# A new order of issue and new buffer slots for a fused LSH attention and mixing kernel on one core

## The chip, the cores and the metric

The kernel runs on one core of one Trainium2 chip. The metric is device microseconds of an execution. The kernel before has a median of 711.25 us over 3 runs (711.11 to 713.57).

## What is computed

The reference has two parts. Attention runs for 4 batches, 8 heads, 768 positions and head size 64. Each query and key gets a 6-bit bucket from the signs of its product with `proj`; a query sees only the keys of its own bucket.

```python
mask = q_bucket[:, :, :, None] == k_bucket[:, :, None, :]
scores = np.where(mask, scale * np.matmul(q, k.transpose(0, 1, 3, 2)), -1000000000.0)
attn = np.exp(scores - np.max(scores, axis=-1, keepdims=True))
out = np.matmul(attn / (np.sum(attn, axis=-1, keepdims=True) + 1e-09), v)
```

The heads of a batch are laid side by side (768 x 512, called x below), and a mixing block follows:

```python
theta = x @ w_theta
y = einsum('ts,bsd->btd', w_tok_r, x * cos(theta)) + einsum('ts,bsd->btd', w_tok_i, x * sin(theta))
u = x + y
return u + np.maximum(u @ w_ch, 0.0)
```

## The kernel before, in words

Products are made to a precision near float32 out of float16 matmuls: an operand is split into a high and a low half, and a product takes three matmuls. So most stages have a step that makes the high half, one that subtracts it to get the low half, and groups of three matmuls.

**Attention.** For each batch and each pair of heads, `prep_qk` (line 443) loads queries and keys, scales and splits them and makes the rows of bucket bits (`sign`); `prep_v` (line 326) does the same for values. `assemble` (line 565) puts one head's operand together in `qk` by DMAs, and by four small steps that copy or mask the bit rows (`fbit`, `fmask`, lines 584 to 588), which any of ACT, DVE and POOL can do. `maxima` (line 605) computes scores of queries by keys (`qmax`, tile `sq`, PE), takes row maxima on DVE (`vmax`, tile `mc`, line 632), turns them on PE (`mtr`, tile `pmx`), and puts them into the operand by a DMA. `step` (line 677) then computes the scores again, keys by queries (`st`, PE), exponentiates them on ACT (`pf`, line 713), takes the high half on ACT (`p1`, tile `p`, line 719), the low half on POOL (`p2`, tile `p`, line 725), and multiplies by the values (`pv`, tile `po`, PE). One head of the first pair of each batch instead multiplies in float32 without a split. In batches 2 and 3 every second head takes another way (`turned`, line 804): scores `bt`, maxima `bm`, and a transposing DMA of the exponentials. `finish` (line 765) divides by the sums and writes x.

**Mixing.** `moe` (line 909) works on six row tiles of 128 rows for each batch. For each it makes high and low halves of x (`xh`, `xl`, tile `s_x`), turns them by a transposing DMA (`xturn`) and multiplies by `w_theta` (`proj`, tile `ps_th`). Angles are brought into range (`turns`, `rest`, `mag`), sine and cosine come from ACT (`trig`, lines 1086 and 1087), and x times these is split (`zf`, tile `f`, line 1098; `zh`, line 1103 or 1105; `zl`, line 1109). The token sum is 12 groups of 3 matmuls for each row tile (`y`, tile `py`), is added to x (`u`, line 1137), split and turned again (tiles `s_u`, `t_u`), multiplied by `w_ch` (`proj`, tile `ps_r`), and ends with `relu`, a sum (`fin`, line 1153) and a store. The very last row tile turns its data on PE instead (`turned_tile`, line 1007). The mixing of batch 0, 1 and 2 runs among the attention of the later batches; that of batch 3 is the tail.

**Weights** (`prep_weight`, line 236; `prep_wtok`, line 275) arrive as float64 bits and are converted on DVE, ACT and POOL (tiles `w_t`, `wf_t`, lines 212 to 230 and 296 to 301) in the first 260 us.

**The order.** None of these functions issues anything. Each one only registers steps (`op`): a name, the engines that may do it, the steps it depends on, and the buffer slots it uses. There are 4,219 steps. `issue_all` (line 111) first gives each slot a buffer number from the string `SLOTS`, 1,907 digits in the order in which the steps first name the slots; then it walks the string `ORDER` and issues the steps. An entry is an engine's letter (P is PE, A is ACT, D is DVE, G is POOL, S is the queue of DMAs on SyncE) and the step's number in base 36:

```python
for line in ORDER.split():
    e, x = line[0], int(line[1:], 36)
    o = ops[x]
    o.alts[ENGINES[e]][1]()
```

Each engine works through its own entries strictly in this order; a step whose input or buffer is not ready holds up all that stand behind it on the same engine. The first step that uses a buffer waits for all readers of the buffer's last contents.

Of the kernel before, what the change touches and what calls it, by code (L numbers as in the profile page):

```python
# [32 lines left out]
def lsh_attention_moe_kernel(ctx: ExitStack, tc: tile.TileContext, q, k, v, proj, w_theta, w_tok_r, w_tok_i, w_ch, out):  # L33
# [1233 lines left out]
    "0000000000000000000002100021012022110022100010000020001011000110011011101031000011021100221103021013311022111002030031313121300021"  # L1267
    "3010111320011200010110101001111110001110031000101203122211310003121001220331123000211121013010200010200003200010011112011010010101"
    "1031021003102213100203013110120123130010102001200121103021110210011031011101000000111001001211112313001212103100231212012110000333"
    "0221112100300011213100013000010010110010001111100011110012301121023013031111023200201303021111221130300110030022213130030110112121"  # L1270
    "1100100100100100000130111011100011100111001011203231130003111220303021002031032211311210000303220231110010130001230003100011001101"
    "0111010100111020120030020103221230112203010313103002221110110220230030111221201003013130111200011010001011013111010000110013311021"
    "0112213311222000301100031112202313132201001013020001311022030010130001100000001010110010103223102311000002212130322023111131000100"
    "0100301011021003202112313112100003011111022001101111111001200213011311122000003230100132310111232001032331032120022030101311010301"
    "1130210002200011011110011121032311100113301111000113113000222001300020102113103113302002201001203012130011113001330101101001301013"
    "3110010221031120003310113012212010012313210003200213100322000003300011200010300021110111011101111320033003220230003013130001032211"
    "3000032210110310112013102112103221010320111000001231111101100300113301301322001300011330120101221013100302310101111012121110300002"
    "2100331300011100003110110110101113031122010111220013032202011230101301002301110323010132100021012100101233111030001100011110000100"
    "2220113003131301133010221110021200230200013011122313300013020100231111103200001211020012110200111121012202210122000122110130020211"
    "0200100310210010320101101001021031012221012001201031121010222003011101000301110200003111000032113211010010211120212100300021002101"  # L1280
# [4 lines left out]
A6b D6v P6k D6l Sa9 A7b Sab P6i D6j A7d G7g A76 D6c G6d P6o A7f D6p P6s D6t Aaa S7c P6y D6z G6e P6m D6n P6q D6r P6w Aac Pad D6x P6f Dae G7e  # L1285
# [208 lines left out]
```

## Time and profile before

| | |
|---|---|
| median of 3 runs | 711.25 us |
| span of the profiled execution | 709.1 us |
| around the span, against the median | 2.15 us |
| PE busy / matmuls | 664.1 us / 6,212 |
| DVE busy | 599.4 us |
| ACT busy | 587.7 us |
| POOL busy | 419.8 us |

The span is that of one profiled execution, from its first to its last instruction. Busy time of an engine is the time in which at least one of its instructions runs. A matmul's row is longer than the time that it keeps the next one from starting: consecutive rows overlap, so busy times of PE are to be read by stretches and not by adding rows. An engine that lacks busy time in a stretch was waiting there.

### The profile page before, as it was taken

The numbers are of one execution on the slowest core, as the hardware profiler recorded it, in microseconds if no ns is written. First come the engines' busy times: TensorE is split into PE (matmuls) and PEld (weight loads), VectorE is DVE, ScalarE is ACT, GpSimd is POOL, SyncE is SP. The second block draws the span as 40 slices with busy tenths as digits, with TensorE's granted clock in tenths as the row PEclk, the third lists the DMA queues.
The fourth block names the chain that finished last, engine by engine and source line by source line (L and its number), as shares of the span: only waits on it lengthen the run. The fifth ranks groups of instructions, "written<-read, shape, count | busy, mean of one in ns | idle before, by whom it ended". The sixth has DMA issues, their size and how long they took to land.

```text
span 709.1 us, 16736 instructions
## 1 busy us (share of the span) xinstructions
PE 664.1 (94%) x6212; PEld 391.6 (55%) x6212; DVE 599.4 (85%) x1311; ACT 587.7 (83%) x1043; POOL 419.8 (59%) x411
## 2 busy tenths in 40 slices
PE   3899898899989989999999999999999999999997
PEld 1477675755444555655545565655545565654443
DVE  6899999999999999989998888889997777688222
ACT  7899899999968889999888999999897888875012
POOL 6457677366636567788738879767445778721001
PEclk9999999999999999999999999999999999999999
DMA  6654677657255633368824997888843576960123
GB/s 213 153 143 118 190 177 187 199 110 175 72 132 149 153 87 79 98 165 163 149 70 90 179 178 160 183 188 160 146 109 66 103 158 105 158 132 25 31 59 104
DMA packets 174561, 94.23 MB, mean 133 GB/s; under 512 B 148240, under 2 KB 164240, under 8 KB 174480
## 3 DMA queue, kind: packets, MB, share of 16 engines
q1 hardware_dynamic: 174336, 93.14, 58.1%
q8 instruction: 49, 0.80, 0.5%
q14 instruction: 32, 0.26, 0.1%
q10 hardware_dynamic: 144, 0.03, 0.1%
HBM read 32.53 MB, written 6.29 MB: 55 GB/s over the span
## 4 chain that ended last, share of the span: by engine, by line
PE 45%; DVE 19%; ACT 9%; issue 3%; DMA 0%; POOL 0%; ACTq 0%; DVEq 0%; POOLq 0%
PE py L77 18%; PE po L77 7%; PE ps_r L77 6%; PE st L77 5%; PE bt L77 3%; PE sq L77 2%; DVE f L1098 2%; PE ps_th L77 2%; DVE mc L632 2%; ACT pf L713 1%; ACT z L1086 1%; DVE bm L836 1%; DVE z L1064 1%; ACT pf L864 1%; ACT z L1087 1%
## 5 line engine op out<-in xcount | busy, mean ns | idle before, releaser
L725 POOL TENSOR_TENSOR p<-pf,p 128x512 f16<-128x512 f32 x180 | 226.4, 1272 | 84.8 <-ACT p L719 54.4
L77 PE MATMUL py<-z,wtk 128*128 128x512 f16 x864 | 205.4, 380 | 2.6 <-DVE z L1064 1.6
L632 DVE TENSOR_REDUCE mc<-sq 128x1 f32<-128x512 f32 (+1 forms) x216 | 143.6, 682 | 11.9 <-PE sq L77 10.5
L77 PEld LDWEIGHTS <-qk 120*128 120x128 f16 (+2 forms) x1056 | 98.4, 101 | 89.3 <-issue 28.8
L713 ACT ACTIVATE pf<-st 128x512 f32<-128x512 f32 x216 | 124.4, 590 | 14.8 <-PE st L77 9.3
L77 PEld LDWEIGHTS <-wtk 128*128 128x128 f16 x864 | 82.7, 98 | 93.3 <-issue 5.1
L77 PE MATMUL st<-qk 120*128 120x256 f16 (+1 forms) x576 | 127.0, 330 | 4.3 <-ACT pf L713 3.5
L878 POOL TENSOR_TENSOR late<-pf,late 128x384 f16<-128x384 f32 x96 | 93.6, 987 | 51.2 <-ACT late L872 34.9
L719 ACT ACTIVATE p<-pf 128x512 f16<-128x512 f32 x180 | 110.1, 627 | 6.4 <-PE po L77 4.8
L77 PEld LDWEIGHTS <-p 128*128 128x128 f16 x2160 | 85.2, 98 | 20.4 <-ACT pf L713 1.2
L77 PE MATMUL sq<-qk 120*128 120x512 f16 (+1 forms) x288 | 81.5, 337 | 12.4 <-DVE mc L632 5.0
L77 PE MATMUL po<-vv,p 128*128 128x65 f16 (+1 forms) x2160 | 92.0, 193 | 0.1
L864 ACT ACTIVATE pf<-bt,bm 128x384 f32<-128x384 f32 x96 | 60.7, 664 | 15.0 <-DVE bm L852 10.2
L77 PE MATMUL ps_r<-wch,t_u 128*128 128x512 f16 x276 | 68.2, 379 | 0.8 <-DVE rows L523 0.8
L77 PE MATMUL ps_th<-wth,t_x 128*128 128x512 f16 x288 | 68.2, 379 | 0.6 <-DVE rows L523 0.6
L836 DVE TENSOR_REDUCE bm<-bt 128x1 f32<-128x384 f32 x96 | 50.8, 548 | 14.3 <-PE bt L77 11.4
L872 ACT ACTIVATE late<-pf 128x384 f16<-128x384 f32 x96 | 47.9, 517 | 0.9
L1137 DVE SCALAR_TENSOR_TENSOR x<-py,sw,x 128x512 f32<-128x512 f32 x24 | 17.9, 744 | 31.9 <-PE py L77 31.8
L77 PEld LDWEIGHTS <-t_x 128*128 128x128 f16 x288 | 27.5, 98 | 30.4 <-issue 1.4
L77 PE MATMUL bt<-qk 120*128 120x384 f16 x192 | 43.7, 326 | 0.2
L1098 DVE SCALAR_TENSOR_TENSOR f<-x,zsc,z 128x512 f32<-128x512 f32 x48 | 40.6, 863 | 3.0 <-ACT z L1087 1.8
L77 PEld LDWEIGHTS <-t_u 128*128 128x128 f16 x276 | 25.8, 97 | 28.3 <-issue 2.1
(179 smaller groups left out, 1070.5 us busy)
## 6 DMA issues: line engine op xcount, KB each, us to landing
qk<-hl SPq DMA_DIRECT2D x62, 192.0 KB
raw<-in_k_dram SPq DMA_DIRECT2D x16, 384.0 KB
raw<-in_q_dram SPq DMA_DIRECT2D x16, 384.0 KB
vb<-in_v_dram SPq DMA_DIRECT2D x16, 384.0 KB
out_dram<-x SPq DMA_DIRECT2D x24, 256.0 KB
qk<-hl SPq DMA_DIRECT2D x62, 96.0 KB
w_t<-in_moe_w_tok_r_dram SPq DMA_DIRECT2D x6, 768.0 KB
w_t<-in_moe_w_tok_i_dram SPq DMA_DIRECT2D x6, 768.0 KB
```

The lines of the kernel that those rows point to most:

```text
L77: PE.matmul(out_, l, r, start=start, stop=stop, skip_group_check=True)
L632: DVE.tensor_reduce(col()[:, cs], u["sq"], AX.X, ALU.max)
L713: ACT.activation(wide("pf", spf, F32), u["st"], AF.Exp, scale=1.0 / (UNIT * math.sqrt(D)))
L719: ACT.activation(o_, u["pf"], AF.Copy)
L725: return lambda: eng.tensor_tensor(wide("p2", sp2, F16), u["pf"], u["p1"], ALU.subtract)
L836: DVE.tensor_reduce(part(y), w["w"], AX.X, ALU.max)
L864: ACT.activation(w["f"], w["w"], AF.Exp, bias=part(4), scale=part(3))
L872: ACT.activation(dst(0), w["f"], AF.Copy)
L878: return lambda: eng.tensor_tensor(dst(1), w["f"], dst(0), ALU.subtract)
L1064: DVE.scalar_tensor_tensor(t["zw"][1][:, tt], u["n"], t["mg"], res["ps"], ALU.subtract, ALU.subtract)
L1098: DVE.scalar_tensor_tensor(u["f"], tl[b][:, tt], zsc[:, b : b + 1], t["zw"][r][:, tt], ALU.mult, ALU.mult)
L1137: DVE.scalar_tensor_tensor(tl[b][:, to], res["py"], t["sw"][:, to : to + 1], tl[b][:, to], ALU.mult, ALU.add)
```

## The change

The two strings are replaced: every place in the walk, and 1,085 of the 1,907 slot digits. The set of steps, the functions behind them and the pools of buffers stay. Cut to its first and last lines:

```diff
 SLOTS = (
-    "0000000000000000000002100021012022110022100010000020001011000110011011101031000011021100221103021013311022111002030031313121300021"
...
-    "120211312003200011001102003011100031001111022112200120211003201120110220110011111003010"
+    "0000000000000000000001010120101212012202100010000022000101110010111010100111000031021113321123120000110332022011031020303111210031"
...
+    "132001310101031020000100103211100030100201002102011220121103101112110220110001111103000"
 )
 ORDER = """
-S5i A0 D1 S5g P5w D5x S64 A5j A5h P5k D5l A65 P66 D5m D5n D5o D5p A60 D67 A5z D5q D68 A62 D5r A5y S2 D5u A61 D5s D5v A63 P6u D69 D5t A77 D6a
...
-G35y P37y P37z P380 P381 P382 D370 P38l P38m P38n P383 P38o P38p P38q S2zc A32h P384 P385 P386 P387 P388 P37q P38r P38s D371 P38t D389 S372
-A38a P37r P37s P37t A37u G37v P373 P374 D38b S35z P38u P38v P375 S38c P376 D38w P38y A38z D390 S36m P38d P38e A377 D378 S379 G32i S32j P391
-P392 S37w P393 A394 D395 P38f S396 P38g A38h D38i S38j
+A0 S5i S5g S64 S2 S2k D1 A5j P5w A5h D5x P5k A65 D5l D5m G7g D5n D5o A5z D5p P66 D5q D5r D63 A5u G7d D67 D60 G7e A5s D68 D5v A61 D69 D5y Sab
...
+P37z P380 P381 P36y P37q D36z P37r A370 P382 D371 P383 S372 P384 P38k P38l P37s P37t P38m A37u P373 P374 P38n P38o P385 P386 P387 P388 P38p
+D389 P38q D37v A38a P375 D38b P38r S38c P38s P376 S37w P38t A377 S35z P38u G378 P38v P38d D38w S379 P38e P38y P38f A38z P38g D390 P391 A38h
+P392 G38i P393 S38j A394 D395 S396
 """
```

By engine, the ranks of the steps that stay on their engine move by this many places in its own queue: PE 3.8 on the mean (1,187 of 1,362 move, at most by 35), DVE 3.3 (at most 40), ACT 2.2 (18), POOL 1.1 (7), SP 1.4 (189 of 276, at most 15). 161 steps have another engine's letter. In brackets, how many of them stand among the first 217 us of matmul work in the list of before:

| from, to | steps |
|---|---|
| ACT to DVE | 47 (12): xh 13, fmask 11 (3), mag 9 (3), zh 6 (2), fbit 4 (2), qkh 2, fhi 1 (1), first 1 (1) |
| DVE to POOL | 41 (13): zl 16 (3), fbit 12 (4), fmask 7 (5), fin 5, wmul 1 (1) |
| DVE to ACT | 36 (10): zh 11 (2), fmask 8 (1), fbit 6 (3), xh 5 (1), mag 3, qkh 2 (2), first 1 (1) |
| POOL to DVE | 21 (8): zl 10 (3), fin 5, fbit 3 (2), wmul 2 (2), fmask 1 (1) |
| ACT to POOL | 11 (5): fbit 6 (2), fmask 5 (3) |
| POOL to ACT | 5 (1): fbit 4 (1), fmask 1 |

## Rows read from the trace of the kernel before

**Rows 1.** The page: span, and busy time of each engine with its share.
```profile
span 709.1 us, 16736 instructions
...
PE 664.1 (94%) x6212; PEld 391.6 (55%) x6212; DVE 599.4 (85%) x1311; ACT 587.7 (83%) x1043; POOL 419.8 (59%) x411
```

**Rows 2.** Windows: busy us (x instructions) by engine in seven stretches, TensorE clock, DMA.
```profile
0.00:20.00 20.00, 7.85 (x24) 2.71 (x24) 12.99 (x34) 14.41 (x23) 12.89 (x35) 1.00 0.71 209
20.00:114.00 94.00, 87.76 (x883) 63.45 (x883) 89.46 (x193) 86.32 (x163) 60.71 (x55) 1.00 0.60 166
114.00:147.00 33.00, 29.13 (x310) 21.77 (x311) 32.60 (x78) 32.62 (x61) 16.61 (x16) 0.95 0.63 159
147.00:256.00 109.00, 100.49 (x866) 54.95 (x866) 106.48 (x196) 94.44 (x165) 63.74 (x53) 0.98 0.49 124
256.00:400.00 144.00, 137.63 (x1384) 80.29 (x1383) 132.69 (x293) 133.45 (x237) 102.17 (x94) 1.00 0.59 124
400.00:640.00 240.00, 238.08 (x2454) 139.52 (x2453) 198.71 (x483) 212.18 (x379) 158.30 (x158) 1.00 0.73 144
640.00:709.00 69.00, 63.19 (x296) 28.95 (x294) 26.50 (x40) 14.31 (x22) 5.34 (x5) 1.00 0.18 50
```

**Rows 3.** Waits of PE: for whom, us in total, times, longest.
```profile
PE pb L77 <- DMA raw<-in_q_dram: 5.4, 1, 5.4
...
PE sq L77 <- DVE mc L632: 5.0, 10, 1.0
```

**Rows 4.** Timeline near 255.6 us: start, us, engine, instruction, idle before.
```profile
255.60 0.38 PE L77 MATMUL sq<-qk 120*128 120x512 f16 x1 [0.88 <-DVE cinv_ch L181]
```

**Rows 5.** Timeline near 253 us, DVE and POOL.
```profile
252.97 1.72 DVE L980 SCALAR_TENSOR_TENSOR s_u<-x,su,s_u 128x512 f16<-128x512 f32 x1
...
252.99 1.16 POOL L725 TENSOR_TENSOR p<-pf,p 128x512 f16<-128x512 f32 x1 [1.32 <-ACT p L719]
```

**Rows 6.** Groups of DVE by form, 0 to 256 us: busy us, mean ns, idle.
```profile
L632 DVE TENSOR_REDUCE mc<-sq 128x1 f32<-128x512 f32 x84 | 56.5, 680 | 1.0 <-PE sq L77 0.6
...
L1098 DVE SCALAR_TENSOR_TENSOR f<-x,zsc,z 128x512 f32<-128x512 f32 x12 | 11.6, 964 | 0.8 <-ACT wg_ch L222 0.7
...
L586 DVE TENSOR_SCALAR qk<-rows,pp 24x384 f16<-24x384 f16 x13 | 7.4, 567 | 0.4
...
L301 DVE TENSOR_TENSOR wf_t<-wf_t 128x768 f16<-128x768 f32 x12 | 13.4, 1127 | 0.1
...
L226 DVE SCALAR_TENSOR_TENSOR wf_t<-wf_t,scw 128x1536 f32<-128x1536 f32 x6 | 12.0, 2002 | 0.1
```

**Rows 7.** Tiles, whole run: shortest/median/longest ns, first and last start, forms.
```profile
L632 DVE TENSOR_REDUCE mc<-sq x216: 637/681/693, 13.3 to 585.2; 128x1 f32<-128x512 f32 x73, 128x2 f32<-128x512 f32 x35
...
L1098 DVE SCALAR_TENSOR_TENSOR f<-x,zsc,z x48: 730/747/1751, 171.3 to 651.4; 128x512 f32<-128x512 f32 x48
...
L586 DVE TENSOR_SCALAR qk<-rows,pp x27: 312/397/1221, 27.6 to 588.5; 24x384 f16<-24x384 f16 x27
...
L301 DVE TENSOR_TENSOR wf_t<-wf_t x12: 936/958/1941, 84.5 to 238.7; 128x768 f16<-128x768 f32 x12
...
L226 DVE SCALAR_TENSOR_TENSOR wf_t<-wf_t,scw x6: 1797/1818/2687, 74.8 to 234.3; 128x1536 f32<-128x1536 f32 x6
```

**Rows 8.** Groups of POOL, whole run: busy us, mean ns, idle and its releasers.
```profile
L725 POOL TENSOR_TENSOR p<-pf,p 128x512 f16<-128x512 f32 x180 | 226.4, 1272 | 84.8 <-ACT p L719 54.4 <-PE po L77 8.1 <-issue 7.4
...
L586 POOL TENSOR_SCALAR qk<-rows,pp 24x384 f16<-24x384 f16 x4 | 6.3, 1566 | 0.4
```

**Rows 9.** Timeline of the tail.
```profile
694.83 1.23 SPq L984 DMA_TRANSPOSE t_u<-s_u  x1
...
699.30 0.64 PEld L77 LDWEIGHTS <-t_u 128*128 128x128 f16 x4
...
704.85 0.69 ACT L1150 ACTIVATE rl<-ps_r,qu 128x512 f32<-128x512 f32 x1 [0.61 <-PE ps_r L77]
...
705.57 0.69 DVE L1153 TENSOR_TENSOR x<-rl,x 128x512 f32<-128x512 f32 x1 [0.60 <-ACT rl L1150]
```

More of the change, by code (lines that the diff above doesn't have):

```diff
@@ L1271 @@
[L1271 to L1278, printed above, removed]
@@ new lines @@
+    "1021110300011000010010101101110001100311011111000023033203111123100003121231102130110011311100200011000002300010011010001100011110"
+    "1110030323001202310023130011120231132311000031013001102131110030011021011100010101100110100311112210311312000002231322013302001011"
+    "1210003110201130012000121000030010110010001101001010110122001333120000111122120013330011133001221101102200203013200110223130011320"
+    "1111300123100110001000010011011011130010300123200110223132012320001111200110122300300112130112230130001213211000230001010010101101"
@@ new lines @@
+    "0111110100121113000012113012031212130001330221000213103013103101023013110101233032112021110000013000010101012101111000012001213101"
+    "0030211210202123313100021110212210001003021133121001211002031000331000220002211110010002103022112211110020212331211100201200333101"
+    "1100300000021003212112313101120013001111011001220111001011301320201021011033313111133001102021020001233301022121132231001100110210"
+    "0233210000100003110011100111033331011013301020333121112330020010210121130003001103322111220113201110113011101001010110000111101020"
@@ new lines @@
+    "1003302021111032013121103123100201002330300001201112110123301002011133200011100032110110100001133110111212030331121101020020033300"
+    "1110122032003121001000012332103113011221111030001330110001100200120312111033111103021020033112131002100200021113231021120110201001"
+    "3301021100010000023010011001001122011313103110021210011110001322023300001032012011001230112302001231110323111032001201100100111201"
+    "2110002212330100001111220013132110002010231101321302301311100301302210011000001211320010113000121120122112021012010312012031112200"
@@ L1282 @@
+    "2130032111100011010030110200310110103110221020120231012201111011031002201002101100010210201131000100221131020210102021311101100120"
+    "132001310101031020000100103211100030100201002102011220121103101112110220110001111103000"
 )
 ORDER = """
[L1284 to L1285 removed]
@@ new lines @@
+Phd Ahj Pgz Pem Dh0 Ad Gkf D2y Sgj Pep Ahk Dke Ahe Ghl Dfq Pgv Ab Phn Dgw Sh Pi2 Ahf Dkg Pes Aho Dc Sf Ghg Ai3 Ph3 Phs Dh4 Ahp Pgt Pdz Aht
+Dgu Pki Ghq Pi7 Ak0 Det Dh7 Phx Deu Ph8 Dkj Phh Ai8 Pku Ahu Dha Po7 Dh9 Shc Dkv Pkk Ahy Pih Ghv Do8 Ai4 Phm Do9 Dkl Pky A2z Pic Doa Shb Gi5
+Dob De0 Ahz Pk1 Doc De1 Phr Sl6 Aid Dk2 Dod Pkw De Gi0 Poj Ala Dkx Ai9 Phw Aii Pir Dk3 Dk4 Dkz Pkm Aie Gia Pi1 Dkn Sg Ais Pkq Pio Dl9 Aij
+Gl8 Pko Pi6 Dk5 Dl7 Aip Gif Pj9 S32 Doe Dok Ak6 Piq Dkr Gik Aoh Dkp Pj6 Pib Dk7 Aja Pks Pig Aj7 Doi Gk8 Piu Aof Pix Dkt St9 Pit Aiv Di A30
@@ new lines @@
+Px9 Ay0 Gxi P10f A4a Pxe Dzw D10g Szy Pxu A49 P2no Dzx D4v A14c Gxn D10i P2np A2e D4b P2o4 Axr D4w S4o Pyv D2f A14e P10b Gxs P2o5 A2g Dyw
+Dyx Pxj Dyy D10c Pxo Axv S2i Dyz P2o6 D2h Az0 P10d P2nq D13s Ay5 S2j P10y A4x Dz1 Axw P118 Ay1 P107 Gxx Pxt D108 S18j A119 P2o7 S14b D4p
+A11a P2o8 Gy2 D10e Ay6 P10t D4q A4r P2o9 A10u Gy7 D2nr P109 A4y P2oa D10a Szz A14d P10j G4z P2op D2iq A14f Gz2 P2oq A18k P105 Pxy Py3 A4s
+P11i A10z Py8 D2io D106 P2or A10v A11j Dy9 P2os D4t G11b A110 D50 Dya P10l P2ob A2mi D51 D52 D10m Gz3 P53 A2lv P11s P113 D2lw G10w A11t Pz4
```

272 lines of the change are left out of this document (130 added, 142 removed).

## The prediction

> **What bounds the kernel now.** I read the page first [rows 1]. PE (the matmul engine) is busy for 664.1 of 709.1 us, so 45.0 us of the span are without a matmul. A new order cannot shorten the matmuls; it can only win from those 45.0 us, or lengthen them. Next come the windows [rows 2], where the reader should look at PE and DVE side by side. PE lacks 12.2 us in the first 20, 6.2 from 20 to 114, 3.9 from 114 to 147, 8.5 from 147 to 256, then only 6.4 from 256 to 400 and 1.9 from 400 to 640, and 5.8 in the tail. DVE is the reverse: from 20 to 256 us it lacks only 4.5 + 0.4 + 2.5 = 7.4 of 236 us (97% busy), and after 400 it has room (198.7 of 240). So there are two regimes: up to 256 us DVE is the engine that is always full and PE waits for it here and there; after 256 PE is full itself. The waits agree: apart from the first load (5.4 us, once) PE waits longest and most often with the score matmul `sq` behind the row maximum `mc` on DVE, 5.0 us in 10 waits [rows 3].
>
> How far DVE binds can be counted along the orders. For a matmul group, add the durations of all DVE instructions up to the last one that it needs, and subtract the matmul work that stands ahead of it on PE: PE must have been idle at least that long. In the order of before the largest value is at the `sq` group that begins at 255.60 us [rows 4]: 240.7 us of DVE against 216.4 us of matmuls, 24.3 us. (The DVE sum agrees with the windows: 13.0 + 89.5 + 32.6 + 106.5 = 241.6 up to 256 [rows 2].) PE's real idle time by then is 30.8 us. What the floor doesn't explain is DVE's own idle time, 7.0 us in the first 20 and 7.4 after.
>
> Against this reading speaks the Trainium skill (Perfetto Trace Analysis, Identifying the Most-Contended Engine): it says that matmul busy time is a poor measure of the distance to the limit, that weight-load busy time is a better one, and that the engine with the highest occupancy is the one to improve. By that rule PE would have room (weight loads 55%) and DVE, 85%, would bind throughout. The windows side with the rule up to 256 us and against it from 400 to 640, where PE has 1.9 us left.
>
> **The change part by part.** All 4,219 steps stay; 161 change engine, nearly all others stand a few places from where they stood (on PE by 3.8 places on the mean, at most 35), and 1,085 of 1,907 buffer slots differ.
>
> *DVE's floor.* Counting the new order by the same durations (a step that changes engine gets the mean of its kind on its new engine), the largest value is 241.4 us of DVE against 218.2 of matmuls: 23.1 us. **Gain 1.2 us.** Of it 0.9 is work that leaves DVE ahead of that point (23 steps leave, 20 come: the table of the change has them); the rest is order. Bounds: 0 (the mean durations don't hold) and 1.2.
>
> *DVE beside POOL.* The same DVE instruction takes different times. At 252.97 us `s_u` takes 1.72 us beside a POOL subtraction [rows 5]. In the first 256 us the mean of `f` is 964 ns, of the mask copy `qk` 567, of the two weight steps `wf_t` 1127 and 2002 [rows 6]; their shortest are 730, 312, 936 and 1797 [rows 7]. The surplus is 12 x 0.23 + 13 x 0.26 + 12 x 0.19 + 6 x 0.21 = 9.7 us. The row maxima `mc`, which read PSUM, lie between 637 and 693 in all 216 cases [rows 7]; so it is instructions that read SBUF alone which suffer. I therefore counted, for each POOL step up to the 218th us of matmul work, which DVE steps the list sets beside it: SBUF-only ones for 56.6 us of 145.8 before, 49.9 of 156.0 after. That is 12% less time, or 18% less as a share. **Gain 12 to 18% of 9.7, taken as 1.5 us.** The other end is a loss: POOL gets 11.4 us more work ahead of 256 us, 7.9% of its 144.6, and if collisions grow with POOL's time, 0.8 us are lost. Upper end 1.7.
>
> On these collisions the Trainium skill (SBUF — State Buffer, SBUF: two separate sides) says that VectorE and GpSimd share one port pair as an exclusive lock, held for a whole instruction, and that the loser stands still until the other ends. The `s_u` row agrees in kind: 1.72 us is 1.0 over the 0.7 that steps of its size take elsewhere (`f` in rows 7), and POOL's subtraction takes 1.16. By the lock alone, more POOL work is more lost DVE time, and this part would be a loss.
>
> *DVE's own idle time, 7.4 us.* For each matmul group I took its latest producer on another engine and asked how much matmul work the list sets between the two, less the producer's duration; negative values are matmul work that is lacking. Summed from 0 to 20, 120 and 220 us of matmul work they are 22.8, 18.7 and 12.1 us for the order in which before really started its steps, and 28.3, 24.5 and 9.5 for the new list. The early part is no better, the later one is. I take **0**, between -7.4 (all of it goes) and +4.5 (it doubles in 20 to 114).
>
> *PE's waits from 256 to 640, 8.3 us [rows 2].* The same count gives 15.6 and 9.7 before (220 to 400, 400 to 600 us of matmul work), 9.2 and 10.9 after: 20% less. **Gain 1.7 us**, between 8.3 and -3.
>
> *ACT and POOL.* ACT loses 10.7 us of work and POOL gains 30.2 over the span. Both have cover: up to 640 us POOL is busy for 16.6 of 33 us at its emptiest and 102.2 of 144 at its fullest [rows 2]. If the cover went, a step moved to POOL would cost what it holds up the subtraction `p` behind it (third rival). ACT alternates between the exponential and the sine 12 times in either order, so table loads cost the same.
>
> *SP's queue.* 189 of 276 steps change rank, by 1.4 places on the mean, and carry their DMAs with them. No DMA step stands over 15 places away, and PE's only long wait for one is the first load. Cost 0.
>
> *The tail.* Before ends with the project of row tile 4, after with that of tile 5; either way the last matmul is followed by one ACT step and one DVE step of 0.69 us each [rows 9] and a store. Tile 4's last sum moves to POOL (1.27 us, as the equally wide `p` [rows 8]): covered by the 12 matmuls left, 12 x 63.2/296 = 2.6 us [rows 2]. Tile 4's way from its token sum through ACT, DVE and a transposing DMA had slack; now 9 groups of 3 matmuls (27 x 0.2135 = 5.8 us) stand beside 3 steps of about 0.7 and a DMA that is issued at 694.83 and read at 699.30 [rows 9], at most 4.5. At worst 0.8 us are uncovered; I take 0.
>
> **Sum.** -1.2 - 1.5 + 0 - 1.7 + 0 = -4.4. The profiled execution spans 709.1 us, which is 2.15 below the median of the runs, 711.25; so 704.7 spanned, and **706.8 us** as a median, 0.6% faster. Half a per cent (3.6 us) is about what a measurement of this kernel can tell from no change, so the forecast lies only just outside.
>
> **The rivals.**
> *The stalls go too.* If the new order also takes 5.0 of DVE's 7.4 us and 3 more of the 6.6 us left of PE's waits after 256, the time is 706.8 - 8.0 = 698.8. For it: from 120 us of matmul work on, producers stand earlier. Against: ahead of that they don't.
> *DVE's total is what counts.* By mechanism: DVE stays 97% full, and what is gained at one group is waited for at the next. DVE's work falls by 1.7 us over the span, so 709.6; if POOL's extra work lengthens collisions by 0.8 as well, 710.4. This is what the skill's rule on the most-contended engine and its port lock would give together. For it: the floor moves by only 1.2. Against: PE's windows after 256.
> *POOL holds up the subtraction.* 18 steps go to POOL ahead of 256 us; a mask step takes 1.57 us there against 0.57 on DVE [rows 6, 8]. The subtraction `p` behind it, which the next `po` matmuls read, has 84.8/180 = 0.47 us of idle time ahead of it [rows 8], so each such step can delay PE by 1.1 us where PE is right behind. Four of them eat the gain; from 8 on the kernel is slower by over 0.5%. With 9 it is 706.8 + 9.9 = 716.7. Against: POOL is half empty from 114 to 147 us.
>
> **How the numbers follow.** Forecast as summed 0.42, stalls gone too 0.13, DVE's total 0.30, POOL 0.15. Faster by over 0.5% (below 707.7) are the first two: 0.55; the third is no change: 0.30; the fourth slower: 0.15. The range is to leave out 2 in 10: it ends at 699.5, short of the centre of the best case, and at 714.0, which takes in the forecast with DVE's idle time doubled (711.3) and the third rival's lighter half.
>
> **What would show it.** Right: up to 256 us PE lacks some 3 us less than 30.8, DVE stays over 96% full, and the means of `f` and `wf_t` fall. From 256 to 640 PE lacks 6 to 7 us in place of 8.3. Wrong: DVE's busy time in that stretch falls by over 5 us (collisions were worth more), or its idle time changes by more than 3 (the order itself counts), or PE's waits name POOL's `p` or `qk`.

## The result, and the profile after

The new kernel takes **717.68 us** as a median of 10 executions (715.4 to 723.88); the kernel before, run beside it on the same chip, 712.64 (711.11 to 715.85). The ratio is 1.0072, 95% interval [1.0047, 1.0098]: slower by 5.0 us, where 4.4 us less were forecast and 714.0 was the upper end of the range. The profiled execution spans 715.3 us, against 709.1 before. One execution of e12 and one of e15 below fell into a slower state and are left out of their times.

The page of the new kernel answers to [rows 1]:

```profile
span 715.3 us, 16724 instructions
...
PE 670.2 (94%) x6212; PEld 393.8 (55%) x6212; DVE 607.2 (85%) x1302; ACT 581.0 (81%) x1026; POOL 453.6 (63%) x437
```

PE has the same 6,212 matmuls and is busy for 6.1 us longer with them. POOL has 33.8 us more (30.2 by the durations of before) and ACT 6.7 less; DVE, which by the durations of before should have 1.7 us less, has 7.8 more. The windows, in the stretches of [rows 2] (columns as there: busy us and instructions of PE, PEld, DVE, ACT, POOL, then TensorE's clock, DMA share, GB/s):

```profile
0.00:20.00 20.00, 7.88 (x26) 3.10 (x26) 12.73 (x34) 13.03 (x21) 14.90 (x35) 1.00 0.70 234
20.00:114.00 94.00, 89.74 (x880) 64.37 (x880) 87.09 (x186) 82.46 (x156) 62.43 (x60) 1.00 0.53 144
114.00:147.00 33.00, 29.38 (x277) 22.22 (x276) 30.81 (x73) 29.29 (x53) 15.64 (x17) 0.90 0.73 193
147.00:256.00 109.00, 98.79 (x874) 54.06 (x873) 105.49 (x187) 95.81 (x165) 67.98 (x52) 0.98 0.55 127
256.00:400.00 144.00, 138.05 (x1387) 79.94 (x1384) 135.88 (x299) 129.70 (x232) 109.38 (x99) 1.00 0.56 120
400.00:640.00 240.00, 237.07 (x2459) 138.63 (x2457) 203.00 (x481) 209.51 (x373) 174.28 (x172) 1.00 0.73 144
640.00:715.30 75.30, 69.31 (x323) 31.44 (x321) 32.16 (x45) 21.21 (x30) 9.01 (x7) 1.00 0.20 51
```

Read DVE first. From 20 to 256 us it lacks 6.9 + 2.2 + 3.5 = 12.6 us, where it lacked 7.4; it is 95% full in place of 97%. PE lacks 30.2 us up to 256 (30.8 before) and 8.9 from 256 to 640 (8.3 before). So PE does not stand still longer; it works longer. Look at the clock in 114 to 147: 0.90, in [rows 2] 0.95.

The cleanest place to compare is one matmul that waits for DVE in both kernels: the total of the channel weights, `pw_ch`. First its row in the kernel before and the window up to it, then the same of the new kernel:

```profile
251.91 0.38 PE L77 MATMUL pw_ch<-wcol_ch,ones 128*128 128x1 f32 x2 [0.97 <-DVE wcol_ch L258]
...
0.00:251.91 251.91, 222.03 (x2065) 141.32 (x2066) 237.54 (x489) 224.29 (x400) 150.94 (x153) 0.99 0.57 153
```

```profile
259.27 0.38 PE L77 MATMUL pw_ch<-wcol_ch,ones 128*128 128x1 f32 x2 [0.82 <-DVE wcol_ch L258]
...
0.00:259.27 259.27, 228.24 (x2068) 144.85 (x2068) 239.33 (x488) 223.46 (x397) 164.14 (x164) 0.98 0.57 148
```

It comes 7.4 us later. By DVE's account, 1.8 us of that are more work (237.5 to 239.3) and 5.6 more time without work (14.4 to 19.9; counted instruction by instruction, as the expectations below do, 14.8 to 20.3). By PE's account, 1.1 us are more idle time (29.9 to 31.0) and 6.2 more busy time for 2,068 matmuls in place of 2,065. At the usual pace of each form of matmul the work ahead of this one is 214.6 us in place of 213.7, so 5.3 of the 6.2 are the same work done at a slower pace (the half clock, shown below, can account for 4.9 of them at most).

(In [rows 4] the largest value of the prediction's floor was at the scores at 255.60 us; in the new kernel it is at `pw_ch`.) Behind it 1.2 us come back in this execution: the two executions differ by 6.2 us in span, the medians by 5.0. In a second profile of the new kernel (e16 below) `pw_ch` begins at 258.83 us, and the time behind it is 457.6 us, 457.2 in the kernel before. So the loss lies ahead of this matmul.

What DVE waited for from 20 to 256 us (for whom: us in total, times, longest), before and after:

```profile
DVE mc L632 <- PE sq L77: 0.9, 3, 0.4
```

```profile
DVE mc L632 <- PE sq L77: 5.9, 14, 1.5
DVE wf_ch L212 <- DMA w_ch<-in_moe_w_ch_dram: 1.3, 1, 1.3
```

Most of what is new is the row maximum `mc` waiting for scores `sq` (4.0 us in 11 waits in the second profile). [Rows 3] has the other direction, PE's scores waiting for the maxima; it rose too, and a wait of PE for transposing DMAs is new (whole span):

```profile
PE sq L77 <- DVE mc L632: 8.1, 17, 1.8
...
PE ps_th L77 <- DMA t_x<-s_x: 1.7, 4, 0.7
```

The groups of DVE up to 256 us, as [rows 6], and the subtraction on POOL over the span, as [rows 8]:

```profile
L632 DVE TENSOR_REDUCE mc<-sq 128x1 f32<-128x512 f32 x82 | 54.7, 679 | 3.9 <-PE sq L77 3.5
...
L301 DVE TENSOR_TENSOR wf_t<-wf_t 128x768 f16<-128x768 f32 x12 | 12.4, 1037 | 0.1
L226 DVE SCALAR_TENSOR_TENSOR wf_t<-wf_t,scw 128x1536 f32<-128x1536 f32 x6 | 12.3, 2055 | 0.1
L1098 DVE SCALAR_TENSOR_TENSOR f<-x,zsc,z 128x512 f32<-128x512 f32 x12 | 11.1, 921 | 0.2
...
L1109 DVE TENSOR_TENSOR z<-f,z 128x512 f16<-128x512 f32 x9 | 7.7, 852 | 0.1
...
L586 DVE TENSOR_SCALAR qk<-rows,pp 24x384 f16<-24x384 f16 x11 | 6.6, 603 | 0.3
...
L1067 DVE TENSOR_SCALAR z<-z 128x512 uint32<-128x512 uint32 x6 | 4.5, 747 | 0.0
```

```profile
L725 POOL TENSOR_TENSOR p<-pf,p 128x512 f16<-128x512 f32 x180 | 228.9, 1287 | 94.3 <-ACT p L719 71.1 <-issue 8.0 <-PE sq L77 5.0
```

Two of these groups, which [rows 6] does not show, in the kernel before:

```profile
L1109 DVE TENSOR_TENSOR z<-f,z 128x512 f16<-128x512 f32 x9 | 6.1, 681 | 0.0
...
L1067 DVE TENSOR_SCALAR z<-z 128x512 uint32<-128x512 uint32 x3 | 1.2, 416 | 0.0
```

The collisions beside POOL did not go; they moved. `f` fell by 43 ns for each of 12 and L301 by 90 for each of 12, 1.6 us; L226 rose by 53 for each of 6, `qk` by 36 for each of 11, L1109 from 681 to 852 (9 instructions) and L1067 from 416 to 747 (6): together 4.2 us more. Other groups fell, among them L216 and L212 of `wf_t` by 148 and 118 ns for each of 6. Over all forms of DVE instructions that both kernels have, the changes of the means up to 256 us add up to 0.6 us more (7.7 up, 7.1 down).

The end is that of [rows 9], with the other row tile: one ACT step, this DVE step, and the store.

```profile
711.74 0.69 DVE L1153 TENSOR_TENSOR x<-rl,x 128x512 f32<-128x512 f32 x1 [3.29 <-ACT rl L1150]
```

### The profile page after: what moved, and what is told of

Its sections match the earlier page's. It is cut to its first block, busy times and chain, and to the rows that moved or that the text cites. A ratio compares the mean times of both kernels' runs of the same rounds, so it can differ in the third digit from the quotient of the medians.

```text
span 715.3 us, 16724 instructions
## 1 busy us (share of the span) xinstructions
PE 670.2 (94%) x6212; PEld 393.8 (55%) x6212; DVE 607.2 (85%) x1302; ACT 581.0 (81%) x1026; POOL 453.6 (63%) x437
## 4 chain that ended last, share of the span: by engine, by line
PE 56%; DVE 28%; DMA 6%; ACT 5%; issue 3%; POOL 1%; SPq 0%; DVEq 0%; ACTq 0%; POOLq 0%
PE py L77 19%; PE po L77 11%; PE st L77 7%; DVE mc L632 7%; PE ps_r L77 6%; PE bt L77 4%; PE sq L77 4%; DVE f L1098 3%; PE ps_th L77 2%; DVE z L1064 1%; PE pb L77 1%; DVE hl L473 1%; DMA qk<-row 1%; DMA t_x<-s_x 1%; DVE wf_t L226 1%
## 5 line engine op out<-in xcount | busy, mean ns | idle before, releaser
L725 POOL TENSOR_TENSOR p<-pf,p 128x512 f16<-128x512 f32 x180 | 228.9, 1287 | 94.3 <-ACT p L719 71.1
L632 DVE TENSOR_REDUCE mc<-sq 128x1 f32<-128x512 f32 (+1 forms) x216 | 144.2, 680 | 18.4 <-PE sq L77 17.4
L77 PE MATMUL st<-qk 120*128 120x512 f16 (+1 forms) x576 | 128.6, 331 | 5.6 <-ACT pf L713 3.6
L878 POOL TENSOR_TENSOR late<-pf,late 128x384 f16<-128x384 f32 x96 | 95.4, 1005 | 36.3 <-ACT late L872 29.4
L77 PEld LDWEIGHTS <-p 128*128 128x128 f16 x2160 | 86.7, 99 | 19.5 <-issue 4.1
L77 PE MATMUL sq<-qk 120*128 120x512 f16 (+1 forms) x288 | 83.0, 340 | 15.1 <-DVE mc L632 8.1
L77 PE MATMUL po<-vv,p 128*128 128x65 f16 (+1 forms) x2160 | 93.9, 195 | 0.4 <-POOL p L725 0.4
L1153 POOL TENSOR_TENSOR x<-rl,x 128x512 f32<-128x512 f32 x8 | 10.1, 1268 | 56.2 <-ACT rl L1150 56.2
L1098 DVE SCALAR_TENSOR_TENSOR f<-x,zsc,z 128x512 f32<-128x512 f32 x48 | 44.6, 942 | 0.4
L1109 POOL TENSOR_TENSOR z<-f,z 128x512 f16<-128x512 f32 x20 | 26.6, 1334 | 28.9 <-ACT z L1103 17.4
```

Of the source, the lines that this page charges most:

```text
L77: PE.matmul(out_, l, r, start=start, stop=stop, skip_group_check=True)
L632: DVE.tensor_reduce(col()[:, cs], u["sq"], AX.X, ALU.max)
L725: return lambda: eng.tensor_tensor(wide("p2", sp2, F16), u["pf"], u["p1"], ALU.subtract)
L878: return lambda: eng.tensor_tensor(dst(1), w["f"], dst(0), ALU.subtract)
L1098: DVE.scalar_tensor_tensor(u["f"], tl[b][:, tt], zsc[:, b : b + 1], t["zw"][r][:, tt], ALU.mult, ALU.mult)
L1109: return lambda: eng.tensor_tensor(t["z"][r, 1][:, tt], u["f"], t["z"][r, 0][:, tt], ALU.subtract)
```

## The experiments

Each was timed against the kernel before on the same chip, whose median was 712.9 to 713.6 us. "DVE without work" is counted up to `pw_ch` (the expectations call it the wall matmul): 14.8 us before, 20.3 in the new kernel. Times are medians; a ratio comes from all executions that are compared and need not be the quotient of two medians (for e18 that would be 1.0025).

### The three parts of the change, one alone

The order with the old engines, and the other way round:

```diff
 e1, from the new kernel: the 161 steps back on their engines
-G7d D67 D60 G7e A5s D68
+A7d D67 A60 G7e D5s D68
 e2, from the kernel before: the 161 steps on their new engines
-A60 D67 A5z D5q D68 A62 D5r A5y
+D60 D67 A5z D5q D68 A62 D5r D5y
```

> The new list and the new slots, but each of the 161 moved steps back on its old engine. If the engine moves cost the time (POOL 30 us fuller, its subtractions later), the time is within 1.5 us of the kernel before. If the new order itself costs it, the time stays 4 to 6 us above before. By the trace of the changed kernel the second is likelier: PE's new waits up to 130 us are for DVE row maxima and ACT exponentials, none for POOL.

> The old list and the old slots with the 161 steps on their new engines. Engine moves to blame: 4 to 6 us above before. Order to blame: within 1.5 us of before.

Measured: e1 746.02 us (ratio 1.0462, [1.0444, 1.0481]), e2 742.95 (1.0437 [1.0406, 1.0468]). All four forecasts fell. Either part alone costs 30 to 33 us, six times what both cost together, so neither can be called the cause of the 5 us. An order fits one choice of engines.

Then the buffer slots. The prediction gave them no term at all.

```diff
 e9, from the kernel before: slots of the new kernel where they are free
-30101113200112000101101010011111
+31211103000110100101101011001100
 e10, from the new kernel: slots of before where they are free
-10211103000110000100101011011100
+30111103200112000101101010011111
```

> The order and the engines of before, with the buffer slots of the new kernel wherever the old order leaves them free (1,052 of the 1,907 slots differ from those of before, 395 had to be chosen anew). Slots theory (other buffers make a step wait for another reader, and that is where the 5.0 us come from): 715 to 718 us, ratio 1.004 to 1.007, and DVE without work up to the wall matmul goes from 14.8 us towards 20. Order theory (the slots only follow the order): within 1.5 us of before, ratio 0.998 to 1.002, and DVE without work at 14 to 16 us.

> The order and the engines of the new kernel, with the slots of before wherever the new order leaves them free (358 of 1,907 had to be chosen anew, where the new kernel differs in 1,085). Slots theory: most of the loss goes, 713 to 715 us, ratio 1.000 to 1.003. Order theory: as the new kernel, 716 to 719 us, ratio 1.005 to 1.009, and DVE without work up to the wall matmul stays at 19 to 22 us.

Measured: e9 770.21 (1.078 [1.0742, 1.0817]), e10 751.09 (1.0527 [1.0508, 1.0546]). Both expectations fell, by far more than the whole change. DVE without work is 37.8 us in e9 and 29.1 in e10. PE waits for its score buffers' last readers, in e9 and then in e10 (waits of the whole span):

```profile
PE st L77 <- ACT pf L713: 21.9, 23, 2.0
PE sq L77 <- DVE mc L632: 14.0, 20, 2.1
```

```profile
PE sq L77 <- DVE mc L632: 24.3, 38, 2.5
PE st L77 <- ACT pf L713: 8.8, 16, 1.9
```

So which buffer a step gets decides as much as where it stands, and a set of slots fits one order. Both runs price a mixed set, since 395 and 358 slots had to be chosen anew. In the new kernel, slots and order fit better: its row for `st` behind `pf` is 3.6 us in 4 waits (3.5 in 6 before), and for `sq` behind `mc` the 8.1 shown above (5.0 before). How much of these 3.1 us more the slots hold, and how much the order, these runs don't show.

### Stretches of the new list in the old one

```diff
 entries of ORDER (4,219), with their slots
 e3:  1 to 923 new, the rest old            (until 120 us of matmul work)
 e4:  1 to 923 old, the rest new
 e5:  1 to 1563 old, the rest new           (until 220)
 e6:  924 to about 1590 new, the rest old
 e7:  1564 to 3890 new, the rest old        (220 to 560)
 e12: 205 to about 640 new, the rest old    (20 to 80)
```

> The new list (order, engines, slots) until 120 us of matmul work have been issued, the old list after. In the traces PE's idle time of the new kernel is 4.0 us ahead of the old one's at that point and 6.2 at the end. If the loss is made there and carried along: 3 to 5 us above before. If what is lost early is won back in a stretch where DVE has room: within 1.5 us.

> The complement: the old list until 120 us of matmul work, the new list after. If the loss is made early: 1 to 3 us above before (the 2.2 us that the traces add after that point). If it is made anywhere by the denser order: 4 us or more above before.

> The old list until 220 us of matmul work, the new one after. Theory: the loss arises where DVE binds, because DVE itself has to wait there more often than before (19.9 us idle up to 256 us against 14.5), so the part after 220 costs little: within 1.5 us of before, or 1 us faster, since PE's waits from 220 to 400 were 0.8 us shorter in the new trace. Rival, the loss is spread over the later list as well: 2.5 us or more above before, as in the complement before (4.7 us with the new list from 120 on).

> The new list only between 120 and 220 us of matmul work, the old one on both sides. Theory: 2 to 4 us above before, since this is the DVE-bound stretch in which the runs so far differ. Rival, the loss is spread: at most 1 us above.

> The new list only between 220 and 560, where PE binds; old before and after, so without the new tail, which costs 1.2 us in both traces that have it. Theory: 0 to 2 us faster than before. Rival: 1 us or more slower, because a seam or the later list costs time of its own.

> The new list (order, engines, slots) only from 20 to 80 us of matmul work, the one stretch in which PE lost less time in the new kernel than in any kernel with the old list (2.0 against 2.5 to 4.1 us), and the list of before ahead of and behind it (26 slots chosen anew). If that stretch is better in itself: 711 to 712.5 us, ratio 0.997 to 0.999, faster than both kernels. If what it saves is given back behind it, or at its two seams: 713 to 716 us, ratio 1.000 to 1.004.

| kernel | us | ratio, 95% interval |
|---|---|---|
| e3 | 714.21 | 1.0018 [0.9999, 1.0036] |
| e4 | 716.72 | 1.0065 [1.0044, 1.0087] |
| e5 | 716.84 | 1.0048 [1.0034, 1.0063] |
| e6 | 715.86 | 1.0039 [1.0018, 1.0060] |
| e7 | 720.52 | 1.0108 [1.0084, 1.0132] |
| e12 | 721.25 | 1.0113 [1.0085, 1.0140] |

e3 came as if the loss were won back later, e6 as its theory has it; in e4, e5 and e7 the second case or the rival came, and e12 lies above both of its cases. No stretch of the new list is shown to be faster than the old one, and no single one costs all that the whole list costs: e3, e6 and e5 cost 1.3, 2.8 and 3.4 us by their ratios, 7.5 in sum (with intervals of 1 to 1.5 us each way) where the whole costs 5.1. e12 shows why such sums don't hold: 60 us of the new list, in which it lost least, cost 8 us when they are set in, more than the whole new list. A seam needs slots of its own (26 in e12, 49 in e7, where PE loses 7.2 us, over its matmuls at their usual pace, behind 560 us of matmul work and 1.7 in the kernel before; up to 1.5 of it in a stretch at half clock from 621.6 to 625.0 us) and leaves the steps behind it out of turn. The profiles say where such a cost sits: behind `pw_ch` e5 takes 461.0 us, where the kernel before takes 457.2 and the new one 456.0 and 457.6. So e5's loss belongs to its seam or to what follows it, and does not speak for a loss of the whole list there. These six runs don't divide the loss.

### Scores earlier, maxima later

```diff
 e8, from the new kernel: 114 scores up to two places earlier on PE
-P6m A7a Pad G7f D6n P6w
+P6m A7a P6w Pad G7f D6n
 e11, from the new kernel: 99 maxima one place later on DVE
-D6r P6k D6l Aac P6s D6c P6y
+D6r P6k Aac P6s D6c D6l P6y
```

> The whole new list, but up to 220 us of matmul work the score matmuls that DVE reduces (sq) stand up to two places earlier on PE, 114 of 127 of them. In the new trace DVE waited for sq 5.9 us between 20 and 256 us in 14 waits, against 0.9 in 3 before. If these waits are what was lost: 2 to 5 us faster than the new kernel, about level with before. If they only mirror PE's own lateness: PE then waits for the two buffers of sq instead, and the time stays or rises by some us.

> The new kernel, in which 99 of the 127 row maxima up to 220 us of matmul work stand one place later on DVE. Theory that DVE stands still since the list sets the row maximum too close behind its scores: the 17.4 us that DVE waits for the scores fall by 4 us or more, DVE without work up to the wall matmul falls from 20.3 to 16 to 18 us, 713 to 716 us. Rival, that DVE's maximum and the next scores follow each other through two banks, so that a later maximum only holds up the scores: PE's waits for the maxima rise from 8.1 us to 11 or more, DVE without work stays at 20 or over, 718 to 723 us.

Measured: e8 722.05 (1.0129 [1.0104, 1.0155]), e11 726.44 (1.0180 [1.0162, 1.0197]). In both the waits that were aimed at became less, and the time more. Whole span, DVE and PE, for e8 and then e11; the new kernel has 17.4 us in 33 waits and 8.1 in 17:

```profile
DVE mc L632 <- PE sq L77: 12.9, 22, 1.4
...
PE sq L77 <- DVE mc L632: 17.5, 27, 2.1
```

```profile
DVE mc L632 <- PE sq L77: 13.0, 23, 1.4
...
PE sq L77 <- DVE mc L632: 15.5, 17, 2.5
```

Scores and maxima hand each other two banks. Whether the scores are set earlier or the maxima later, the wait goes over to the other engine: 4.5 us less on DVE are 7 to 9 more on PE. A wait in the table is thus no loss that can be taken out by moving its step everywhere. In e8 the second case of its expectation came. For e11 the rival's waits came (15.5 us on PE, 22.7 of DVE without work), and a time above even its range.

### The clock

In the first profile of the new kernel the full clock (2.4 GHz) comes later and the half clock (1.2 GHz) lasts longer. A score row at half pace and the first at full pace, before and after (start, us; a score matmul of 120x512 takes 0.63 us at half pace and 0.38 at full; the second row of the kernel before is a pair of half the size):

```profile
25.45 0.63 PE L77 MATMUL sq<-qk 120*128 120x512 f16 x1
...
26.80 0.38 PE L77 MATMUL sq<-qk 120*128 120x256 f16 x2
```

```profile
29.11 0.63 PE L77 MATMUL sq<-qk 120*128 120x512 f16 x1
...
32.92 0.38 PE L77 MATMUL sq<-qk 120*128 120x512 f16 x1
```

The clock's records begin at 26.0 and 31.9 us. Behind that, windows ahead of and in the first stretch at half clock, of the kernel before and of the new one:

```profile
128.50:142.00 13.50, 11.84 (x102) 9.62 (x102) 13.33 (x30) 13.28 (x27) 5.69 (x6) 1.00 0.68 213
142.00:145.40 3.40, 3.40 (x22) 2.12 (x22) 3.34 (x8) 3.40 (x8) 2.48 (x3) 0.50 0.54 104
```

```profile
114.00:127.50 13.50, 9.88 (x110) 5.80 (x109) 13.34 (x37) 12.63 (x23) 10.19 (x9) 1.00 0.76 186
127.50:134.30 6.80, 6.80 (x70) 6.24 (x69) 6.76 (x13) 5.98 (x8) 1.00 (x1) 0.50 0.71 184
```

PE has less to do ahead of it (9.9 of 13.5 us, before 11.8), then is at half clock for 6.8 us in place of 3.4, and full all through. DVE's longest wait for scores comes right behind it. DVE's row, and PE's of the work that stood ahead of the scores:

```profile
135.97 0.69 DVE L632 TENSOR_REDUCE mc<-sq 128x1 f32<-128x512 f32 x1 [1.50 <-PE sq L77]
```

```profile
133.20 2.52 PE L77 MATMUL po<-vw,pf 128*128 128x65 f32 x16
135.56 0.38 PE L77 MATMUL sq<-qk 120*128 120x512 f16 x1
```

Up to `pw_ch`, and with the time ahead of the first record counted as half clock, PE works 29.5 us at half clock in this profile and 19.6 in the kernel before. Half of the difference, 4.9 us, is the most that the slower matmuls can cost.

Is this the cause, and can it be had back? e13 and e14 put idle matmuls into PE's first gaps; e15 sets the beginning back; e16 is the new kernel again.

```diff
             o.alts[ENGINES[e]][1]()
+            for _ in range(HEAT.get(x, 0)):
+                if not heat:
+                    heat.append(psum["s"].tile([P, 512], F32, tag="s_0", bufs=1, name="heat"))
+                mm(heat[0], fts[0][:, :P], fts[0][:, :512], True, True)
 e13, new:    HEAT = {222: 9, 246: 1, 250: 1, 238: 1}
 e14, before: HEAT = {222: 8, 236: 2, 250: 1, 248: 2}
 e15: entries 1 to 204 of ORDER old, the rest new
```

> The new kernel with 12 more matmuls (128x128 by 128x512, float16, into a bank that nothing reads before the first scores of the second kind) in PE's gaps from 8 to 19 us: 9 behind the first column total, three single ones behind row-maximum scores. Nothing else is changed. Clock theory (PE is at the half clock until 31.9 us since it has done too little before, and DVE waits for its scores): the full clock comes at 20 to 26 us, DVE's waits at 29 to 33 us (1.3 us) go, and the time falls by 1 to 3 us, to 714 to 716.5. List theory: the clock may come sooner, but DVE waits elsewhere for what it gained, and the time is within 1 us of the new kernel's (716.5 to 718.5) or longer.

> The kernel of before with 13 such matmuls in its own gaps from 8 to 20 us (8 behind the first column total, 2, 1 and 2 behind row-maximum scores). Clock theory: the full clock, which comes at 26.0 us now, comes at 20 to 22 us; the gain is smaller than in the new kernel, 0 to 2 us (711 to 713.5), so that the two kernels come closer together. If matmuls that nothing needs only delay the scores behind them: 713.5 to 716.

> The list of before (order, engines, slots) for the first 20 us of matmul work, and the new list behind it. Clock theory: the full clock comes at 24 to 27 us as in every kernel with the old beginning, and 1 to 3 us of the loss go: 714.5 to 716.5 us, ratio 1.002 to 1.005. List theory (the loss lies in 80 to 220 us of matmul work): within 1 us of the new kernel, ratio 1.006 to 1.009.

> The new kernel once more, unchanged, beside the other three. 716.5 to 718.5 us, ratio 1.005 to 1.009. Clock theory: DVE's waits for the scores that lay in or behind a half-clock stretch stand elsewhere or are shorter where that stretch stands elsewhere; the waits at other places come again. List theory: the same waits at the same scores, the 1.5 us at 136 us among them, wherever the clock falls.

Measured: e13 721.89 (1.0101 [1.0065, 1.0136]), e14 714.20 (1.0017 [1.0000, 1.0035]), e15 726.41 (1.0152 [1.0112, 1.0192]), e16 718.25 (1.0061 [1.0034, 1.0087]). The idle matmuls did lift the clock: its records begin at 15.5 us in e13 and at 13.3 in e14. But it fell again, in e13 at once:

```profile
15.50:18.90 3.40, 2.02 (x10) 0.82 (x9) 3.35 (x7) 1.41 (x4) 0.67 (x1) 1.00 1.00 219
18.90:25.70 6.80, 6.31 (x24) 2.03 (x23) 5.68 (x17) 5.66 (x9) 2.46 (x4) 0.50 0.13 29
```

and in e14 for 6.8 us at 88.3. No time was gained; the 1 to 3 us hoped for in e13 did not come, and e14 lies in the range named for matmuls that only delay the scores. On the idle clock the Trainium skill (TensorE: Matmul & The Clock Gate, What's actually happening) says that the throttled state is the default and that activity releases it; the first record of e13 and e14 agrees. That the clock then stays up, neither run shows.

e16 tells what comes again with the same list. The late first rise does not: the records begin at 23.1 us, and a short stretch at half clock follows. The half clock near 127 us does come again, 6.8 us long and at 125.5, and so does the wait behind it:

```profile
26.50:30.00 3.50, 3.33 (x10) 1.15 (x10) 3.18 (x7) 2.18 (x4) 2.74 (x3) 0.51 0.81 237
...
112.00:125.50 13.50, 10.51 (x115) 6.42 (x114) 13.37 (x35) 13.14 (x25) 11.71 (x9) 1.00 0.77 176
125.50:132.40 6.90, 6.81 (x68) 5.70 (x67) 6.67 (x14) 5.67 (x9) 0.17 (x1) 0.51 0.74 200
```

```profile
134.47 0.69 DVE L632 TENSOR_REDUCE mc<-sq 128x1 f32<-128x512 f32 x1 [1.06 <-PE sq L77]
```

It is 1.06 us here and 1.50 in the first profile, at the same score. Since the stretch at half clock stands at nearly the same place too, e16 cannot tell whether the wait belongs to the clock or to the list. Up to `pw_ch` PE works 27.6 us at half clock here, 8.0 more than in the kernel before. e15 has the half clock at its largest: in its profile PE is at half clock for 13.6 us from 41.1 (PE busy 12.95). Its time is 6 (by the ratios) to 9 us (by the medians) over the new kernel's, against both expectations. At half clock PE works 41.2 us there, 11.7 more than in the new kernel's first profile, which can cost 5.9 us at most.

The sizes can be had from all executions, since each has its mean granted clock. The mean is 0.9937 over 82 executions of the kernel before and 0.9901 over 17 of the new one (these ten and the seven of e16). Within the new kernel, 7 executions at 0.992 or more have a mean span of 714.4 us, 10 below that 717.8. **At equal clock**, 0.992 to 0.993, the mean span is 711.5 us before (29 executions) and 714.5 after (6). So 2.9 of the 5.0 us of difference in span are there at the same clock, and 2.1 go with the lower clock. (The mean leaves out the time ahead of the first record, so the later start at 31.9 us is among the 2.9.)

### Single places

If what is left at equal clock lies in waits that come again at the same steps, moving those steps should bring it back. Eight of PE's steps, whose inputs were there while other matmuls stood ahead, were moved one to five places:

```diff
 e17, from the new kernel (five of the eight)
-A8w D81 Pfb Dbd D82 A9a Pbe S84
+A8w D81 Pbe Pfb Dbd D82 A9a S84
-Sby Dbh P9j G92 Aey Pbq Pba
+Sby Dbh Pbq P9j G92 Aey Pba
-Adh Pcm Pg6
+Adh Pg6 Pcm
-Ann Pn2 Pn7 Aos
+Ann Pn2 Pq3 Pn7 Aos
...
-Pni Dot Pq3 Pns A10
+Pni Dot Pq1 Pns A10
...
-Pnv Dto Pq1 Pnl
+Pnv Dto Pnl
 e18: the same, and from 570 us of matmul work on the old list and slots
```

> The new kernel with eight PE steps one to five places earlier, all of them steps whose inputs were there but which stood behind other matmuls while DVE waited for them: six row-maximum scores that DVE waited for (at 36, 38, 61, 136, 137 and 192 us of the first profile) and their neighbour, and one column total (at 43 us). Together these waits are 3.8 us in the first profile of the new kernel and 3.1 in the second. Single-places theory: DVE without work up to the wall matmul falls from 20 by 3 us, 714 to 715.5 us, ratio 1.001 to 1.004. Rival, as where all scores were set earlier (e8): the steps that were passed are late in their turn, DVE waits as long elsewhere, 717 to 719 us.

> The same eight moves, and the list of before from 570 us of matmul work on (2 slots chosen anew). There the new list sets three projections right behind the transposing DMAs that they read, and PE stands still for 0.4, 0.3 and 0.7 us at 627, 635 and 641 us; the old list has two other matmuls there and no such wait. If that is the 1.2 us: 1.0 to 1.5 us less than e17, and PE loses 1.7 us in place of 2.9 behind 560. If the old end costs as much at its seam: as e17, or longer.

Measured: e17 717.08 (1.0065 [1.0036, 1.0093]), e18 714.96 (1.0049 [1.0024, 1.0074]). In e17's profile the waits did go, from 5.9 us (4.0 in e16) to 2.2 (20 to 256 us). A new one came, in a stretch at half clock that now lies from 139.5 to 149.7:

```profile
DVE mc L632 <- PE sq L77: 2.2, 9, 0.4
DVE rc L775 <- PE po L77: 2.0, 1, 2.0
```

```profile
145.48 0.20 DVE L775 RECIPROCAL rc<-po 128x6 f32<-128x6 f32 x1 [2.05 <-PE po L77]
```

DVE without work fell to 18.4 us, by 1.9 and not 3. `pw_ch` came no earlier for it, at 260.68 us in place of 259.27: DVE's same 488 instructions up to there took 3.4 us longer (242.7 us, 239.3 in the new kernel). At clock 0.992 to 0.993 the mean span is 713.6 us (3 executions, 712.7 to 715.0), 0.9 less than the new kernel's, and of e18 712.7 (4 executions, 712.6 to 712.7), another 0.9 less. Each of the two steps alone is within the scatter of these few executions; both together, 1.8 us, are clear of it (the new kernel's six lie between 713.5 and 715.3). The medians show 0.6 to 1.2 for the eight moves and 2.1 more for the old end, since the clock fell in some executions as before. The profiles do not show where the old end gains. The waits for transposing DMAs, new kernel and e18, from 606 us on, are 1.0 us and, in two rows, 1.1:

```profile
PE ps_th L77 <- DMA t_x<-s_x: 1.0, 3, 0.5
```

```profile
PE ps_th L77 <- DMA t_x<-s_x: 0.7, 1, 0.7
PE ps_r L77 <- DMA t_u<-s_u: 0.4, 1, 0.4
```

The kernel before has no such row there. PE's lost time behind 560 us of matmul work did not fall to 1.7 in e18 (3.2 in its profile, 2.9 in the new kernel), so what e18 gains over e17 rests on the spans alone. No version beat the kernel before.

## Why the prediction was wrong

*DVE's own idle time, "I take 0, between -7.4 and +4.5".* **This is the step that failed.** It rose by 5.6 us up to `pw_ch`, beyond its own upper end. I had counted how far the new list sets producers ahead of the matmuls that read them and found "the early part is no better, the later one is"; from a mixed answer I took no change. Two things were missing. The count looked at what PE waits for and not at what DVE waits for, and the loss came as DVE waiting for PE's scores (0.9 to 5.9 us). And it took every matmul at its usual pace: that the clock could change had no term, though [rows 2] shows 0.95 and 0.98 where DVE binds. Up to `pw_ch` the same matmuls took 5.3 us longer in the profiled execution, at most 4.9 of it by the half clock; over all executions 2.1 us go with the lower clock.

*DVE's floor, "gain 1.2 us".* At the durations of before it falls from 24.3 to 23.1. At the new kernel's own, DVE's 238.8 us (counted instruction by instruction) stand against 214.6 of matmuls at `pw_ch`: 24.2. The floor did not fall. The lower bound named for this case, "the mean durations don't hold", is what happened.

*DVE beside POOL, "gain 12 to 18% of 9.7".* Right in kind for the groups that fell, wrong in sum: others rose by as much, and all forms together took 0.6 us more up to 256 us. The other end, that collisions grow with POOL's time (0.8 us lost), is nearer to what came. Over the span POOL has 33.8 us more work, and DVE 7.8 us more with 9 instructions fewer. The Trainium skill (SBUF — State Buffer, SBUF: two separate sides) has the two engines share a port pair as an exclusive lock that is held for a whole instruction. More lost DVE time beside more POOL work agrees with that in sign.

*PE's waits from 256 to 640, "gain 1.7".* 8.9 us after 8.3: a loss of 0.6.

*SP's queue and the tail, "cost 0".* PE's waits for the transposing DMA behind 606 us, three in the new kernel and none before, 1.0 us in all, stand against it: the old list has two other matmuls ahead of one of these projections, the new one has none. Yet the time behind `pw_ch` is not longer than before, and that setting the end back gains (0.9 us at equal clock) is not clear of noise.

*The rivals.* The third, POOL holding up the subtraction, did not come: PE waits for `p` twice in the whole span, 0.4 and 0.3 us, and never for a mask step on POOL; `p` has 94.3 us of idle time ahead of it, not less than 84.8. The second came nearest in its mechanism ("what is gained at one group is waited for at the next" is what e8, e11 and e17 show), but its price was 709.6 to 710.4. A case in which PE gets slower was not among the rivals, and it should have been.

*The text's own signs* decided: "its idle time changes by more than 3 (the order itself counts)" is what the windows show, 7.4 to 12.6 us. The other sign, DVE's busy time falling by over 5 us up to 256, came too (241.5 to 236.1), but not since collisions were worth more: the new kernel has got less far by then.

**The account**: the loss lies ahead of `pw_ch`, which comes 7.4 and 6.9 us later in the two profiles of the new kernel. There DVE waits longer for PE's scores, and PE works 8 to 10 us longer at half clock. Of the 5.0 us over all executions, 2.1 go with the lower clock; that the clock causes them, and that the list causes the clock, is argued and not shown. Of the 2.9 at equal clock, the eight moves and the old end together took back 1.8 (4 executions against 6), and neither alone is clear of noise. Where they act stays open: `pw_ch` comes no earlier in their profiles (260.7 and 259.2 us). Some 1.1 us are left without a place. The later first rise of the clock is a poor candidate for them, since e16 has the loss without it: up to 30.0 us PE works 14.0 us at half clock there, in the kernel before 13.0 up to 26.0. Whether the new list's thinner PE work at 114 to 127 us makes the clock fall for longer is argued from three profiles in which the two came together (9.9 of 13.5 us ahead in the new kernel, 10.5 in e16, 9.3 in e13); e17, with 12.0 of 13.5 us busy ahead of a stretch of 10.2, speaks against it. It stays open.

## What to carry to other kernels

Order, engines and buffer slots of a list set by a search are one thing: any one of them taken from another list (the slots in part chosen anew) cost 30 to 57 us here, where the whole change cost 5. So price them together, and don't hope to locate a loss by splicing. Where two engines hand buffers to each other and both are nearly full, count waits in both directions, and give the matmul clock a term: a list planned on full-pace durations is not the list that runs when PE falls to half for 7 us. A difference of half a per cent is best read at equal granted clock.

## What the runs showed of the hardware

The clock column of the windows shows 1.00 ahead of the first record, while the rows there run at half pace (`sq` of 120x512 in 0.63 us, 0.38 later); a reader has to look at durations in the first 30 us. The stretches at half clock last between 3.4 and 13.6 us in these profiles. When the same kernel runs again, some come again at nearly the same place and some are new (127.5 and 185.5 us in one profile; 26.5, 125.5, 183.6 and 224.5 in the other), and the first record began at 31.9 us in one and at 23.1 in the other. Lifting the clock early, at 13.3 or 15.5 us, did not make it stay. And a single-input step on SBUF alone, `z` of L1067, went from 416 to 747 ns in the mean up to 256 us as POOL's work grew. Over the new kernel's span the two of 17 that no POOL instruction overlaps take 414 and 417 ns, the other 15 between 405 and 1,399. So steps with one input can suffer beside POOL too.
